# Lightning attention feeding a routed expert layer: where routing's small products stand within a step, and when the first expert's weights are asked for

## The chip, the cores and the metric

The kernel runs on one core of one Trainium2 chip. The figure of merit is device time in microseconds (us), from launch to the last instruction, of one execution; where several executions are given, their median. A profile records one further execution, instruction by instruction; its span (first to last instruction) is a little shorter than the time of that same execution.

The engines are called as in the profile: PE (matrix products; its weight loads are PEld), DVE (elementwise work and scans), ACT (scaling, copies, activations), POOL (elementwise work and indirect DMAs), SP (issues most DMAs). A name with a q, as SPq, is the engine's own instruction queue. Each engine works through its queue in order; between engines, semaphores are the only order.

## The reference

Two blocks. The first is lightning attention over 4 sequences (B), 8 heads, 768 positions and 64 channels; block by block, a decaying state `kv` carries the past:

```python
for b in range(nb):
    intra = einsum('bhic,bhjc->bhij', qb, kb) * Dmask
    intra = einsum('bhij,bhjd->bhid', intra, vb)
    inter = einsum('bhid,bhde->bhie', qb * lam_pow, kv_state)
    out[:, :, sl] = intra + inter
    kv_state = lam_block * kv_state + einsum('bhsd,bhse->bhde', kb * rev_pow, vb)
```

Its output, 3072 rows of 512 values, feeds a layer of 8 experts. Each row gets logits; its expert is the argmax where a local gate is below one half or the sequence begins, and otherwise the expert of the row before it:

```python
e = fresh_e if s == 0 or local_gate[b, s] < 0.5 else prev_e
out[b, s] = p[e] * (maximum(x[b, s] @ w1[e], 0) @ w2[e])
```

Routing is therefore a walk along each sequence, and the expert products can only start on rows whose routing is known.

## The kernel before

Attention runs in 24 steps `s` (`NS` of them): 6 blocks of 128 positions times the 4 sequences, sequence fastest, so that step `s` reads and updates the state of step `s - 4`. In step `s` the queues are filled in this order by hand (line 824 on; PE, DVE, SP and POOL have a manual schedule, ACT's order is the compiler's):

1. `loaded(s + 5)`: SP asks for the step's 1 MB of q, k, v and k again (tile `inp`, 6 buffers; L171).
2. `prepare(s + 3)`: POOL multiplies q by powers of the decay (`qd`, L178) and k likewise (`kd`, L181, not in the last block).
3. If `s` is in `QUARTERS`, SP asks for one quarter (512 KB) of the first expert's first weight matrix, `w1t[0]` (L831). In step 20 it asks for `w2t[0]` (L833) and then, with the routed expert's number, conditionally again (L701, L702); in step 23 for the second expert's (L836, L837).
4. `scores(s + 1)`: PE multiplies k and q of the next step into `ps` (L201 or L209) and DVE masks the result into `sm` (L213, two instructions, one for each half).
5. `from_state(s)`: PE multiplies `qd` with `kv` into `po` (L236); ACT decays `kv` (L240).
6. `logits` in steps 9, 13, 17, 21 (PE L316, DVE L317), then `extra_work(s, 0)`.
7. `gates` in steps 4, 8, 12, 16, 20 (PE L308), then `mix(s)`: PE multiplies `sm` with v into `po` (L249), and ACT copies it to `xc` (L252).
8. `update(s)`: PE multiplies `kd` with v into `pk` (L263); DVE adds that to `kv` (L266). None in the last block.
9. Rows go out to `x_dram`: some are turned by DVE (L294) and written in groups by four SP DMAs (`group_out`, L302; group 2 in step 13); the rows of steps 12 to 19 are turned by PE (L273) a step later and written by an ACT DMA each (L282, from step 13 on).
10. `extra_work(s, 1)`.

`extra_work` calls what the table `extras` has for that step and place. That is how routing is spread over the steps. For the first 8 tiles of rows: `fresh_experts(0)` (step 9: six DVE instructions that end in `mark`, L425), `along_sequences(0)` (PE L433 turns the marks into rows, DVE L436 and L442 carry each expert along its sequence into `run`), `experts_of(0)` (PE L449 turns `run` back, DVE L451 makes one-hot `hot`), `ranks(0)` (step 12; PE L460 and L461 read `hot`). The second part, 4 tiles, follows in steps 13 to 16. `first_tiles` (step 17) and `tokens_to_first_tiles` (step 18) are chains of small DVE instructions (L517 to L542, L558 to L530); in step 19 masks are made (L622 to L485) and multiplied (PE L641), and from the result DVE makes indices (L645 to L650) with which POOL gathers the first rows (L725). `constants_6` is four small ACT copies and two DVE instructions of one column (L377, L378).

After step 23, `first_turned` (PE L734, DVE L735) hands the first gathered tile to the first expert product, `hidden` (L753). From there the expert layer is a long stretch of PE work (L753, L759, L983, L988) to the end.

SP's and ACT's DMAs share eight completion semaphores in turn; a DMA that takes a semaphore over waits in its engine's queue for the DMA that had it before.

Of the kernel before, what the change touches and what calls it, by code (L numbers as in the profile page):

```python
# [37 lines left out]
NA = B * CA  # L38
PARTS = [(0, 8), (8, NA), (NA, NT)]
LOADS = 6  # L40
QUARTERS = [16, 17, 18, 19]
WIDE = [3, 4, 5, 7, 9, 11]
TURNED = {**{r: r + 1 for r in range(3 * B)}, 11: 13, 20: 22, 21: 23, 22: 23}
WARM = 10
# [21 lines left out]
def kernel(  # L66
# [26 lines left out]
    def w1_src(e):  # L93
        return w1[bass.ds(e, 1)].rearrange("o (t p) f -> p (o t) f", p=P)
# [278 lines left out]
    def constants_6():  # L373
        for k in range(4):
            nc.scalar.copy(dupq[:, QP * k:QP * k + QP], ident[:, :QP])
        row = ints[0][:, 2 * P:2 * P + 1]
        nc.vector.tensor_scalar(row, row, P - QP, None, ALU.bitwise_and)  # L377
        nc.vector.tensor_scalar(fourth, row, 1.0 / QP, None, ALU.mult)  # L378
# [19 lines left out]
    def pool(i):  # L398
        return pools[i == 2]

    def hot_of(i):
        lo, hi = PARTS[i]
        return hots[lo // NA][:, :, lo % NA:lo % NA + hi - lo]

    def fresh_experts(i):

        lo, hi = PARTS[i]
        n = hi - lo
        lg = lt[:, lo:hi, :E]
        if not i:  # L410
            nc.vector.memset(lt[0:1, :B, E:], -1.0)
        if i == 2:
            room = rt.tile([P, 2, NA, E], F32, name="each0", bufs=1).rearrange("p k n e -> p (k n e)")
            mx, best, mark = (room[:, n * (E + k):n * (E + k) + n] for k in range(3))
            top, mark = room[:, :n * E].rearrange("p (n e) -> p n e", e=E), mark.bitcast(BF16)[:, :n]
        else:
            mx, best = (rt.tile([P, n], F32, name=f"{k}{i}", bufs=1) for k in ("mx", "best"))
            top = rt.tile([P, n, E], F32, name=f"top{i}", bufs=1)
            mark = rt.tile([P, n], BF16, name=f"mark{i}", bufs=1)
        nows["mx", i], nows["mark"] = mx, mark  # L420
        nc.vector.tensor_reduce(mx, lg, axis=AX.X, op=ALU.max)
        nc.vector.tensor_tensor(top, lg, mx.unsqueeze(2).broadcast_to([P, n, E]), ALU.is_equal)
        nc.vector.tensor_tensor(top, top, down.unsqueeze(1).broadcast_to([P, n, E]), ALU.mult)
        nc.vector.tensor_reduce(best, top, axis=AX.X, op=ALU.max)
        nc.vector.scalar_tensor_tensor(mark, lt[:, lo:hi, E], FRESH, best, ALU.is_le, ALU.mult)  # L425

    def along_sequences(i):

        lo, hi = PARTS[i]
        n = (hi - lo) // B  # L430
        prow = pr[:B, :P * n]
        for c in range(n):
            nc.tensor.matmul(prow[:, P * c:P * c + P], lhsT=nows["mark"][:, B * c:B * c + B], rhs=identb,  # L433
                             start=True, stop=True, skip_group_check=True)
        stay = pool(i).tile([B, P * n], BF16, name=f"stay{i}", bufs=1)
        nc.vector.tensor_scalar(stay, prow, 0.0, None, ALU.is_equal)  # L436
        run = runs[i] = pool(i).tile([B, P * n], BF16, name=f"run{i}", bufs=1)
        before = 0.0
        if i:
            before = rt.tile([B, 1], F32, name="carry", bufs=1)  # L440
            nc.scalar.copy(before, runs[i - 1][:, -1:])
        nc.vector.tensor_tensor_scan(run, stay, prow, before, ALU.mult, ALU.add)  # L442

    def experts_of(i):
        lo, hi = PARTS[i]
        n = hi - lo
        pe = pr[:, P * CA:P * CA + n]
        for c in range(n // B):
            nc.tensor.matmul(pe[:, B * c:B * c + B], lhsT=runs[i][:, P * c:P * c + P], rhs=identb[:B, :B],  # L449
                             start=True, stop=True, skip_group_check=True)  # L450
        nc.vector.tensor_tensor(hot_of(i), pe.unsqueeze(1).broadcast_to([P, E, n]),  # L451
                                down.unsqueeze(2).broadcast_to([P, E, n]), ALU.is_equal)

    def ranks(i):

        lo, hi = PARTS[i]
        n, hot = hi - lo, hot_of(i)
        ptot = pr[:, :E * n].rearrange("p (e t) -> p e t", e=E)
        prank = pr[:, E * NA:E * NA + E * n].rearrange("p (e t) -> p e t", e=E)
        nc.tensor.matmul(ptot, lhsT=onesb, rhs=hot, start=True, stop=True, skip_group_check=True)  # L460
        nc.tensor.matmul(prank, lhsT=beforeb, rhs=hot, start=True, stop=True, skip_group_check=True)  # L461
        tot = pool(i).tile([P, E, n + 1], F32, name=f"tot{i}", bufs=1)
        nc.scalar.copy(tot[:, :, 1:], ptot)
        if i:
            nc.scalar.copy(tot[:, :, 0:1], counts[i - 1])
        else:
            nc.vector.memset(tot[:, :, 0:1], 0.0)
        incl = pool(i).tile([P, E, n + 1], F32, name=f"incl{i}", bufs=1)
        nc.vector.tensor_tensor_scan(incl.rearrange("p e t -> p (e t)"), go[i].rearrange("p e t -> p (e t)"),
                                     tot.rearrange("p e t -> p (e t)"), 0.0, ALU.mult, ALU.add)  # L470
        counts[i] = incl[:, :, n:]
        where = pool(i).tile([P, E, n], F32, name=f"where{i}", bufs=1)
        nc.vector.tensor_tensor(where, prank, incl[:, :, :n], ALU.add)
        nc.vector.tensor_tensor(where, where, hot, ALU.mult)
        rank = pool(i).tile([P, n], I32, name=f"rank{i}", bufs=1)
        with nc.allow_low_precision("whole numbers"):
            nc.vector.tensor_reduce(rank, where.rearrange("p e t -> p t e"), axis=AX.X, op=ALU.add)
        nc.vector.tensor_scalar(place[:, 0, lo:hi], rank, P - 1, None, ALU.bitwise_and)
        nc.vector.tensor_scalar(place[:, 1, lo:hi], rank, -P, None, ALU.bitwise_and)

    def masks(i):

        lo, hi = PARTS[i]
        lane = onehots[i] = (act if i == 2 else route).tile([P, hi - lo, P], BF16, name=f"lane{i}", bufs=1)
        nc.vector.tensor_tensor(lane, countb.unsqueeze(1).broadcast_to([P, hi - lo, P]),  # L485
                                place[:, 0, lo:hi].unsqueeze(2).broadcast_to([P, hi - lo, P]), ALU.is_equal)
# [130 lines left out]
    def brought(i, ks):  # L617

        n, (g0, g1) = NT if i else NA, span(i)
        if 0 in ks:  # L620
            hit = nows["hit"] = pools[i].tile([P, n, g1 - g0], BF16, name=f"hit{i}", bufs=1)
            nc.vector.tensor_tensor(hit, whole[:, g0:g1].unsqueeze(1).broadcast_to([P, n, g1 - g0]),  # L622
                                    nows["to"].unsqueeze(2).broadcast_to([P, n, g1 - g0]), ALU.is_equal)
        hit = nows["hit"]
        if i:
            val = w1t[2].rearrange("p t f -> p (t f)").bitcast(BF16)[:, :n * len(ks) * (g1 - g0)]
            val = nows["val"] = val.rearrange("p (n k g) -> p n k g", n=n, k=len(ks))
        else:
            val = nows["val"] = rt.tile([P, n, len(ks), g1 - g0], BF16, name=f"val{ks[0]}", bufs=1)
        for j, k in enumerate(ks):  # L630
            nc.vector.tensor_tensor(val[:, :, j], hit, parts[:, :n, k].unsqueeze(2).broadcast_to([P, n, g1 - g0]),
                                    ALU.mult)
# [155 lines left out]
    def number(k, n):  # L788
# [2 lines left out]


    extras = {
        (6, 1): constants_2, (7, 1): constants_3, (8, 1): constants_4, (9, 1): constants_5, (10, 1): constants_6,
        (9, 0): lambda: fresh_experts(0), (10, 0): lambda: along_sequences(0), (11, 0): lambda: experts_of(0),
        (12, 0): lambda: ranks(0), (13, 0): lambda: fresh_experts(1), (14, 0): lambda: (along_sequences(1), masks(0)),
        (15, 0): lambda: experts_of(1), (16, 0): lambda: ranks(1), (17, 0): first_tiles,
        (18, 0): tokens_to_first_tiles, (19, 0): lambda: (brought(0, (0, 1)), masks(1)),
        (19, 1): lambda: by_slots(0, (0, 1)), (20, 0): lambda: (ahead(0, 0), ahead(1, 1), rows_out(0)),
        (20, 1): lambda: chances(0), (21, 0): lambda: chances(1), (22, 0): lambda: brought(0, (2, 3, 4)),  # L800
# [6 lines left out]
    with tc.manual_schedule(engines={PE, DVE, SP, POOL}):  # L807
# [16 lines left out]
        for s in range(NS):  # L824
            if s + LOADS - 1 < NS:
                loaded(s + LOADS - 1)
            if s + 4 < NS and s != 1:
                prepare(s + 3)
            if s in QUARTERS:
                j = QUARTERS.index(s)  # L830
                nc.sync.dma_start(out=w1t[0][:, j], in_=w1_src(0)[:, j])  # L831
# [528 lines left out]
```

## Time and profile before

Three executions took 445.30, 445.82 and 443.42 us: median 445.3.

| | us |
|---|---|
| time of the profiled execution | 444.67 |
| its span | 442.9 |
| PE busy (matmuls) | 426.8, 96% |
| DVE busy | 287.7, 65% |
| ACT busy | 194.9, 44% |
| POOL busy | 109.0, 25% |
| first expert product starts | 98.73 |

The page draws engines, clock and DMA in 40 slices of 11.07 us. The first nine slices are attention; the granted TensorE clock was 0.995 of full speed on the mean. Times in the text are microseconds from the span's start. A wait is booked to the engine or DMA that released it last. A piece of a chain of waits is a stretch that set the start of what follows; everything else had slack.

### The profile page before, as it was taken

What the parts mean: (1) busy time and instruction counts of PE and PEld (TensorE: products, weight loads), DVE (VectorE), ACT (ScalarE), POOL (GpSimd) and SP (SyncE); (2) the same over time, 40 slices, a digit from 0 to 9 for tenths busy, and PEclk for the clock granted to TensorE, in tenths of its full rate; (3) what the DMA queues carried; (4) which work ended last, traced back from release to release, by engine and by line L of the source; (5) the groups of instructions that cost most, each with busy time, mean ns of one, the idle gap of its engine ahead of it and who ended that gap; (6) DMA issues with size and microseconds to landing.
All of it is one profiled execution on the core that took longest, in us unless ns stands there. A gap on an engine that the chain in (4) does not pass through costs nothing.

```text
span 442.9 us, 10337 instructions
## 1 busy us (share of the span) xinstructions
PE 426.8 (96%) x4094; PEld 354.4 (80%) x4094; DVE 287.7 (65%) x564; ACT 194.9 (44%) x592; POOL 109.0 (25%) x120
## 2 busy tenths in 40 slices
PE   6999899899999999999999999999999999999993
PEld 6788687677766786978777999667899999898982
DVE  5767997892239959857473785100587879878661
ACT  4245556336455105564234556451455454565110
POOL 4494584420100042205111302200202021020101
PEclk9999999999999999999999999999999999999998
DMA  7999999999999889999993799996164828370101
GB/s 262 410 366 366 361 350 323 348 341 342 347 395 392 294 304 396 399 396 404 394 398 136 255 400 367 343 368 210 40 215 146 314 81 300 128 269 3 55 1 52
DMA packets 48351, 124.84 MB, mean 282 GB/s; under 512 B 3164, under 2 KB 10844, under 8 KB 46368
## 3 DMA queue, kind: packets, MB, share of 16 engines
q1 hardware_dynamic: 42624, 108.03, 66.6%
q0 software_dynamic: 4368, 13.90, 8.9%
q10 hardware_dynamic: 1296, 2.10, 1.3%
q8 instruction: 36, 0.59, 0.5%
q14 instruction: 27, 0.22, 0.1%
HBM read 124.02 MB, written 12.91 MB: 309 GB/s over the span
## 4 chain that ended last, share of the span: by engine, by line
PE 75%; DVE 9%; DMA 8%; issue 6%; POOLq 0%; POOL 0%; ACT 0%; DVEq 0%
PE ps L753 13%; PE pk L759 12%; PE ps L983 12%; PE pk L988 11%; DMA out_dram<-y,sidxp 6%; PE po L983 5%; PE pl L988 4%; PE po L249 3%; DVE sm L213 3%; PE pr L1144 2%; PE pr L1122 2%; PE ps L209 2%; PE pk L263 1%; PE ps L201 1%; PE po L236 1%
## 5 line engine op out<-in xcount | busy, mean ns | idle before, releaser
L753 PEld LDWEIGHTS ps<-xt,w 128*128 128x128 f32 x512 | 58.2, 192 | 3.2 <-issue 2.3
L753 PE MATMUL ps<-xt,w 128*128 128x128 f32 x512 | 59.1, 276 | 0.5 <-DVE xt L735 0.5
L759 PE MATMUL pk<-w,h 128*128 128x512 f32 x128 | 56.6, 594 | 0.0
L759 PEld LDWEIGHTS pk<-w,h 128*128 128x128 f32 x128 | 23.7, 191 | 26.3 <-issue 25.5
L768 POOL DMA_INDIRECT out_dram<-y,sidx x14 | 14.0, 1001 | 105.4 <-DVE y L785 46.5
L725 POOL DMA_INDIRECT xg<-x_dram,gidx x25 | 25.8, 1033 | 56.4 <-DVE lg L739 34.1
L746 ACT COPY xp<-xlast 32x128 f32<-32x128 f32 x128 | 37.8, 296 | 1.7
L213 DVE TENSOR_TENSOR sm<-ps,mask 128x512 f32<-128x512 f32 x46 | 29.5, 681 | 7.8 <-PE ps L201 4.1
L785 DVE TENSOR_SCALAR y<-pk,gate 128x512 f32<-128x512 f32 x8 | 6.0, 744 | 43.9 <-PE pk L759 25.8
L746 ACT COPY xp<-lg 32x128 f32<-32x128 f32 x112 | 33.0, 295 | 2.6
L755 ACT ACTIVATE h<-ps 128x512 f32<-128x512 f32 x16 | 9.6, 597 | 55.2 <-PE ps L753 55.2
L178 POOL TENSOR_TENSOR qd<-inp,lamq 128x512 f32<-128x512 f32 x20 | 25.7, 1285 | 26.2 <-DMA inp<-in_qkv_dram 23.4
L983 PEld LDWEIGHTS ps<-xp,w 128*128 128x128 f32 x256 | 30.5, 192 | 1.6 <-issue 1.3
L983 PE MATMUL ps<-xp,w 128*128 128x128 f32 x256 | 31.3, 276 | 0.0
L983 PE MATMUL ps<-xs,s 128*128 128x128 f32 x256 | 31.2, 275 | 0.0
L988 PE MATMUL pk<-w,h 128*128 128x256 f32 x128 | 30.5, 381 | 0.0
L988 PE MATMUL pk<-s,hsum 128*128 128x256 f32 x128 | 30.3, 380 | 0.0
L249 PE MATMUL po<-sm,inp 128*64 128x128 f32 x384 | 27.9, 280 | 2.3 <-DVE sm L213 1.6
L983 PEld LDWEIGHTS ps<-xs,s 128*128 128x128 f32 x256 | 29.9, 192 | 0.0
L249 PEld LDWEIGHTS po<-sm,inp 128*64 128x64 f32 x384 | 21.0, 136 | 10.1 <-issue 5.8
L988 PEld LDWEIGHTS pk<-s,hsum 128*128 128x128 f32 x128 | 24.0, 190 | 3.2 <-DVE s L1071 0.2
L988 PEld LDWEIGHTS pk<-w,h 128*128 128x128 f32 x128 | 23.6, 191 | 3.3 <-issue 0.6
(282 smaller groups left out, 784.4 us busy)
## 6 DMA issues: line engine op xcount, KB each, us to landing
w<-in_w_dram SPq DMA_DIRECT2D x43, 2048.0 KB, 12.0
inp<-in_qkv_dram SPq DMA_DIRECT2D x15, 1024.0 KB, 10.8
inp<-in_qkv_dram SPq DMA_DIRECT2D x10, 512.0 KB, 8.4
x_dram<-w SPq DMA_DIRECT2D x12, 256.0 KB, 5.7
inp<-in_qkv_dram SPq DMA_DIRECT2D x4, 768.0 KB, 8.2
x_dram<-xn ACTq DMA_DIRECT2D x8, 256.0 KB, 6.8
w<-in_w_dram SPq DMA_DIRECT2D x4, 512.0 KB
x_dram<-inp SPq DMA_DIRECT2D x4, 192.0 KB, 7.8
```

The lines of the kernel that those rows point to most:

```text
L178: nc.gpsimd.tensor_tensor(qd, x[:, 0].rearrange("p (a i) -> p a i", i=P), lamq, ALU.mult)
L209: nc.tensor.matmul(ps[u][half, a, first:], lhsT=kt[rows, a, half], rhs=qt[rows, a, first:], start=True, stop=True, skip_group_check=True)
L213: nc.vector.tensor_tensor(sm[:, u], ps[u], mask[:, u], ALU.mult)
L249: nc.tensor.matmul(head(a, u), lhsT=vn[:, a, u], rhs=sm[:, u, a], start=(not c and a < 2), stop=True, skip_group_check=True)
L725: nc.gpsimd.indirect_dma_start(out=xg, out_offset=None, in_=x_dram[:n, :], in_offset=bass.IndirectOffsetOnAxis(ap=gidx[i][:, j:j + 1], axi ...
L746: copy(xt[QP * j:QP * j + QP, :, QP * k:QP * k + QP], blocks[QP * k:QP * k + QP, :, j])
L753: nc.tensor.matmul(ph[:, j], lhsT=w1t[w][:, d, P * f:P * f + P], rhs=xtt[i][:, d], start=(d == 0), stop=(d == DT - 1))
L755: nc.scalar.activation(hq[half, i], ph, ACT.Relu)
L759: nc.tensor.matmul(pys[i], lhsT=hq[f // 4, i][:, f % 4], rhs=w2t[w][:, f], start=(f == 0), stop=(f == FT - 1))
L768: apart(nc.gpsimd.indirect_dma_start(out=out, out_offset=bass.IndirectOffsetOnAxis(ap=sidx[i][:, j:j + 1], axis=0), in_=y, in_offset=None, ...
L983: nc.tensor.matmul(to[:, m], lhsT=a[:, k, P * m:P * m + P], rhs=b[:, k], start=(new and not m and not k), stop=(k == 1), skip_group_check= ...
L988: nc.tensor.matmul(to, lhsT=a[:, f], rhs=b[:, f], start=(new and not f), stop=(f == FT // 2 - 1), skip_group_check=True)
```

## The change

`along_sequences` and `experts_of` move from place 0 of their steps (ahead of `mix`) to place 1 (after `update` and the rows that go out), for both parts of the rows. `constants_6` is called just ahead of `along_sequences(0)`, in the same place of step 10 as before. `masks(0)` stays in place 0 of step 14. The four quarters of `w1t[0]` are asked for in steps 12 to 15 instead of 16 to 19. Nothing else differs.

```diff
-QUARTERS = [16, 17, 18, 19]
+QUARTERS = [12, 13, 14, 15]
...
-        (6, 1): constants_2, (7, 1): constants_3, (8, 1): constants_4, (9, 1): constants_5, (10, 1): constants_6,
-        (9, 0): lambda: fresh_experts(0), (10, 0): lambda: along_sequences(0), (11, 0): lambda: experts_of(0),
-        (12, 0): lambda: ranks(0), (13, 0): lambda: fresh_experts(1), (14, 0): lambda: (along_sequences(1), masks(0)),
-        (15, 0): lambda: experts_of(1), (16, 0): lambda: ranks(1), (17, 0): first_tiles,
+        (6, 1): constants_2, (7, 1): constants_3, (8, 1): constants_4, (9, 1): constants_5,
+        (9, 0): lambda: fresh_experts(0), (10, 1): lambda: (constants_6(), along_sequences(0)), (11, 1): lambda: experts_of(0),
+        (12, 0): lambda: ranks(0), (13, 0): lambda: fresh_experts(1), (14, 0): lambda: masks(0), (14, 1): lambda: along_sequences(1),
+        (15, 1): lambda: experts_of(1), (16, 0): lambda: ranks(1), (17, 0): first_tiles,
```

In SP's queue the order was load 17, load 18, the four writes of group 2, load 19, load 20, load 21, quarter, load 22, quarter, load 23, quarter, quarter, `w2t[0]`. It becomes load 17, quarter, load 18, quarter, the four writes of group 2, load 19, quarter, load 20, quarter, load 21, load 22, load 23, `w2t[0]` (load `n` fills `inp` for step `n`). POOL's queue is unchanged; PE and DVE execute the same instructions in another order.

## The prediction

> **What bounds the kernel now.** I read the page's slices first, to see which engine is short; then the chain of waits, to see where attention ends late; then the waits around the edited places; then the orders of DVE and POOL where the chain is DVE's.
>
> ```profile
> PE   6999899899999999999999999999999999999993
> DVE  5767997892239959857473785100587879878661
> DMA  7999999999999889999993799996164828370101
> ```
>
> PE is full nearly throughout, and from the first expert product at 98.73 us on it waits 0.5 us in all until 386 (for the first tile, L735). So the expert layer is a block of fixed length, and the change is worth what it does to the start at 98.73. In slices 1 to 9 DVE and DMA are as full as PE; the limit there has to be read step by step.
>
> The chain of waits, 36 to 64 us (start, length, what):
>
> ```profile
> 40.82 0.71 DVE sm L213 x2
> ...
> 44.53 0.81 DVE mark L425
> ...
> 46.75 1.19 DVE sm L213 x2
> ...
> 50.14 1.21 DVE sm L213 x2
> 51.34 0.04 issue
> 51.38 0.79 PE ps L209 x18
> ```
>
> From 40.82 to 51.38 (steps 9 to 12) the chain is DVE's own queue; after that PE's until 72.7 (one stall of 0.72 us at 60.44), then again mostly DVE's until 98.73.
>
> The waits in attention (total us, times, longest):
>
> ```profile
> PE pr L433 <- DVE mark L425: 1.1, 1, 1.1
> ...
> SPq L831 <- DMA x_dram<-xn: 11.1, 3, 8.2
> ```
>
> The first is PE's wait for the marks that the change takes away. The second says that a DMA in SP's queue can be held for a row write of ACT's, whose semaphore it takes over.
>
> DVE, then POOL, in step 17 (start, length, line):
>
> ```profile
> 74.08 1.22 DVE L517 TENSOR_TENSOR more<-incl,whole 128x96 f32<-128x96 f32 x1
> ...
> 75.62 0.61 DVE L537 TENSOR_TENSOR_SCAN ends<-ones,tiles 128x8 f32<-128x8 f32 x1
> ...
> 76.47 1.22 DVE L539 TENSOR_SCALAR ends<-ends 128x8 f32<-128x8 f32 x1
> 77.61 0.16 DVE L540 TENSOR_SCALAR table<-table 128x8 f32<-128x8 f32 x1
> ```
> ```profile
> 73.91 1.28 POOL L178 TENSOR_TENSOR qd<-inp,lamq 128x512 f32<-128x512 f32 x1 [6.02 <-DMA inp<-in_qkv_dram]
> 75.14 1.06 POOL L181 TENSOR_TENSOR kd<-inp,rev 128x512 f32<-128x512 f32 x1
> 76.39 1.27 POOL L178 TENSOR_TENSOR qd<-inp,lamq 128x512 f32<-128x512 f32 x1 [0.18 <-DMA inp<-in_qkv_dram]
> ```
>
> L539 and L540 are the same operation on the same shape: 1.22 and 0.16 us. The long one began just after a POOL product and ended just after it (77.69 against 77.66); so did L517 (75.30, 75.19) and L537 (76.23, 76.20). When POOL's products run is set by when `inp` lands (its bracketed waits). That is how the moved quarters can reach the critical queue, in either direction.
>
> **Part 1: marks and runs behind the update.** Step 10: PE ended `from_state` at 44.64, waited 1.11 us for the marks, then mixed. Now it mixes at once (the mask's result has stood since 42.07): `mix` 1.02 and `update` 0.56 end at 46.2, then L433. But the next thing of PE's that matters, scores for step 12, needs the `ps` that DVE's masking of step 11 releases, 46.67 to 47.94, and DVE comes to that through its own queue, unchanged up to there. After it DVE has the same instructions in another order: before, L436 and L442, then `kv`, the turn L294, L377 and L378; now `kv`, L294, L377, L378, L436, L442. Starts apart: 0.43 + 0.61 + 0.31 + 0.63 + 0.20 = 2.18 us either way, so the next masking starts at 50.05 in both. L433's result, there at 46.5, is wanted at 49.2. Step 11 likewise: `hot` (0.13) goes behind `kv` (0.33) and the turn (0.63), ending near 52.5; the reader, PE's L460, ran at 52.65. Cover: DVE's queue. If it were not the limit, the 1.11 us would be gained; if `hot` came late, up to 0.2 lost. I take 0.
>
> Steps 14 and 15: PE is the limit, and the marks were there (no wait at L433). Its instructions, 0.15 and 0.10 us, stay in the same step: 0. On DVE, `masks(0)` (1.12) now comes ahead of L436 and L442 (0.7): same sum before the next masking at 64.72, and the scores behind that stand at 67.20. Again 0.
>
> **Part 2: the quarters, in bytes.** 58 to 60 us, with loads alone in flight, moved at 414 GB/s: 0.524 MB is 1.27 us, a 1 MB load 2.53. DMA is saturated there, so two quarters ahead of load 19 cost 2.5 us of queue, which the four writes of group 2 and load 19 meet. Coming first they also mean that nothing is gained for `w1t[0]`: it was complete at 92.0 and is needed at 98.73.
>
> **Part 3: the quarters, in semaphores.** In the built program's list of waits one more SP DMA ahead of group 2 moves the turn. Now the third write of group 2 waits for the row write that ACT issues at 59.95, load 19 for the one at 64.48, load 20 for 67.93, load 22 for 72.41. Before, load 19 followed group 2 at 64.98 without such a wait. How long does a row write take? L831's three waits give 67.93 to 76.54, 72.41 to 79.07, 76.34 to 81.74: 8.6, 6.7, 5.4 us, the first behind three loads. For the one at 64.48 the ACT queue's bytes are done by 68, some 4 us. So load 19 goes out between 68.5 and 73.1; I take 70, as it will lie behind group 2's writes, as the short case did, with a quarter's tail more. A load that found the queue nearly dry, load 22, landed 7.1 us after issue with a quarter ahead of it (1.27); so alone 5.8: load 19 lands near 75.8 (bounds 74.3 and 73.1 + 9.2 = 82.3, the longest being that of loads 19 and 20) against 73.9. Load 20, issued near 72 behind a quarter, near 78.5 against 76.3; 21 near 82.5 against 78.95; 22 near 85 against 84.15.
>
> Who waits for load 19? PE's scores at 75.62, then DVE's masking, which started only at 78.42, since DVE was busy until then. Scores take 0.9, so it may land until 77.5 without cost: 1.6 us of slack left. Load 20: scores at 80.16, masking at 82.18, slack about 1 us at 78.5 to 80.3 and more. Load 21: scores at 84.82, 2.3. Load 22: scores at 89.50; its POOL product stands ahead of the gather at 86.22, which may slip by 0.1 to 1 us; the tile that it fetches is wanted at 95.92, and the gather's last bytes moved before 94. I take 0 for lateness; bounds 0 and 82.3 - 77.5 = +4.8.
>
> **Part 4: POOL's products move against DVE.** Steps 17 to 19 lost to such overlaps: L517 1.22 against 0.25 (L520, the like-sized reduction), L537 0.61 against 0.25, L539 1.22 against 0.16, L558 0.92 against 0.35 (L561 over the same elements), L649 0.60 against 0.17: 0.97 + 0.36 + 1.06 + 0.57 + 0.43 = 3.4 us, most of what four products could cost. With load 19 at 75.8, L517 to L542 would run free: eight starts of about 0.2 from 74.08 end at 75.9, `kv` (0.34) at 76.2; the masking then waits for scores, 75.8 + 0.9 = 76.7, not 78.42: a lead of 1.7. Some is lost again: `qd`, `kd` of 19 and `qd` of 20 now run 75.8 to 78.2 and 78.5 to 79.8, over L558 to L530 (eight short ones), up to 1.3; with load 21 at 82.5 its product falls on L622 to L485 (masks, 1.1 us) or on L649. I take back 1.4 of the 1.7: -0.3. Bounds: PE's own work (scores of 21 not before 83.0, if update and row turns follow at once, against 84.82 and a 0.48 stall) gives -2.3 at best; at worst, no lead and one more product's 1.3 lost.
>
> The Trainium skill, "SBUF — State Buffer", section "Who interferes with whom", says that DVE and POOL share one pair of ports as an exclusive lock and that "Issue order, not op shape, decides who blocks." The rows above agree in kind (1.22 against 0.16 us). Its summary would have one schedule off the critical path whichever can wait; this change does not choose, it lets landings decide. By the rule alone the sum would be -3.4 if every overlap went and about 0 if all came back.
>
> **Part 5: later weights.** `w2t[0]` landed at 99.0 and let `w1t[1]` go at 99.16; with the quarters done earlier it may land near 93 to 96. Its first reader is at 108.55, that of `w1t[1]` at 115.67, and PE waits for no weight there: 0.
>
> **Sum.** 0 + 0 + 0 - 0.3 + 0 on a span of 442.9: 442.6. The profiled execution's own time is 444.67 (1.8 around the span), 0.6 under the median of 445.3; I take -0.3 off the median: 445.0.
>
> **Rivals.**
> - *The 1.11 us of waiting for marks were on the path.* For: PE stood still. Against: the chain runs over DVE there. 445.3 - 1.1 - 0.3 = 443.9. Chance 0.09, within 0.5%.
> - *Overlaps mostly vanish.* Loads 19 to 21 land in gaps: -2.3, with the first rival's gain perhaps more: 443.0 down to 441.9. For: 3.4 us are lost to them now. Against: the same products must run somewhere. Chance 0.22.
> - *Loads late behind row writes (slower).* One mechanism: load 19 held for the row write of 64.48, load 20 for that of 67.93. From a landing past 77.5 each us late is a us of path. With the 8.6 us wait and a landing 7.1 after, 80.2: +2.7; at the bound +4.8: 448.0 to 450.1. For: 8.2 us were waited so before. Against: the row writes there were behind three loads. Chance 0.27.
> - *It does nothing*: landings shift within their slack and overlaps even out: 445.3. With the forecast: 0.42.
>
> **Chances and range.** A measurement of this kernel tells about 0.5%, 2.2 us, from no change: 443.1 to 447.5. Faster 0.22, same 0.09 + 0.42 = 0.51, slower 0.27. The forecast's own range, from the middle of the terms, is 443.9 to 446.6. For 8 in 10 I go into both outer cases, leaving one in ten each: 442.1 to 448.6.
>
> **What would show it.** Part 1: no PE wait at L433 in step 10, yet masking of steps 12 and 13 at 50.1 and 52.4 as before. Part 3: SP's waits for row writes move from L831 to L171 and L302, and POOL's wait for `inp` of step 19 ends near 75.8. Part 4: L517 and L539 near 0.2 us, L558 or L485 longer. Part 5: no PE wait for weights. It would be wrong if PE waits for `inp` at L209 in step 18, if the masking of step 12 starts a microsecond earlier, or if the first expert product starts over 2 us from 98.7.

## The result, and the profile after

The changed kernel took 448.0 us (median of 21 executions, 446.25 to 449.81); the kernel before, on the same chip, 445.69 (21 executions, 443.42 to 449.75). The ratio is 1.0063, 95% interval 1.0046 to 1.0080: some 2.8 us slower by the ratio (the two medians lie 2.3 us apart). The profiled execution after has a span of 446.3 us, before 442.9. The first expert product starts at 101.64, before at 98.73: 2.9 of the 3.4 us are lost ahead of it, so what has to be explained is still attention.

Timeline of the kernel after, single engines picked out (start, length, engine, line; in brackets the idle time before it and what ended that):

```profile
46.73 0.27 PE L433 MATMUL pr<-identb,mark 128*4 128x128 bf16 x2
...
75.45 0.25 DVE L517 TENSOR_TENSOR more<-incl,whole 128x96 f32<-128x96 f32 x1
...
75.74 1.27 POOL L178 TENSOR_TENSOR qd<-inp,lamq 128x512 f32<-128x512 f32 x1 [6.58 <-DMA inp<-in_qkv_dram]
...
76.02 1.02 DVE L537 TENSOR_TENSOR_SCAN ends<-ones,tiles 128x8 f32<-128x8 f32 x1
77.07 0.96 DVE L538 TENSOR_TENSOR table<-ends,tiles 128x8 f32<-128x8 f32 x1
78.07 0.17 DVE L539 TENSOR_SCALAR ends<-ends 128x8 f32<-128x8 f32 x1
...
82.11 0.90 PE L209 MATMUL ps<-inp 64*64 64x128 f32 x32 [1.39 <-DVE owner L530]
82.13 1.27 POOL L178 TENSOR_TENSOR qd<-inp,lamq 128x512 f32<-128x512 f32 x1 [4.12 <-DMA inp<-in_qkv_dram]
...
85.92 0.57 PE L209 MATMUL ps<-inp 64*64 64x128 f32 x13
86.04 1.26 POOL L178 TENSOR_TENSOR qd<-inp,lamq 128x512 f32<-128x512 f32 x1 [2.63 <-DMA inp<-in_qkv_dram]
...
88.29 0.60 PE L209 MATMUL ps<-inp 64*64 64x64 f32 x18 [1.80 <-issue]
```

The kernel before, PE at the scores of steps 20 and 21:

```profile
80.16 0.90 PE L209 MATMUL ps<-inp 64*64 64x128 f32 x32
...
84.82 0.56 PE L209 MATMUL ps<-inp 64*64 64x128 f32 x13
85.86 0.61 PE L209 MATMUL ps<-inp 64*64 64x64 f32 x18 [0.48 <-issue]
```

Five things stand in them. PE no longer waits at L433. L517 and L539 are short now (0.25 and 0.17 us, before 1.22 both), but L537 and L538 beside the next POOL products are long (before 0.61 and 0.17). Load 19 landed at 75.74, when POOL's `qd` could start; loads 20 and 21 at 82.1 and 86, against 76.39 and 78.97 before. And PE's scores for steps 20 and 21 start in the same moments as `qd` on these loads: 82.11 and 85.92, that is 1.95 and 1.10 us later than before. Fifth, within the scores of step 21 PE then stood still for 1.80 us, before for 0.48, with no releaser that the profile shows. At 82.11 the wait is booked to DVE's L530, but that began at 81.89, lasts 0.16 us and has nothing to do with `inp`; what ends at 82.1 is the load.

SP's waits, 40 to 125 us (total, times, longest):

```profile
SPq L171 <- DMA x_dram<-xn: 6.9, 3, 4.6
SPq L833 <- DMA x_dram<-xn: 6.0, 1, 6.0
...
SPq L302 <- DMA x_dram<-xn: 4.5, 1, 4.5
```

Before, it was the quarters (L831) that were held for ACT's row writes, 11.1 us in all. Now it is the loads of `inp` (L171), the fourth group's writes (L302) and `w2t[0]` (L833). The chain of waits, 66 to 92 us:

```profile
69.20 6.18 DMA x_dram<-xn
...
75.45 0.33 SPq L171
...
75.82 1.34 SPq L831
...
77.28 8.60 DMA inp<-in_qkv_dram
...
85.92 0.57 PE ps L209 x11
86.49 1.80 issue
```

Read downwards: the row write that ACT issued at 69.20 was done after 6.18 us; only then did SP issue load 20 (75.45), then the fourth quarter (75.82, 1.34 us to issue), then load 21 (77.28), which took 8.60 us, and then PE stood for 1.80 us. In the kernel before, no DMA stands in the chain between 70 and 92 us. So two things delay the loads at once: SP is *held* for a row write, and load 21 *lands slowly*, with a quarter's bytes ahead of it. The experiments try to take these apart.

The late loads are not the whole loss of this one execution. Of the 2.9 us, 1.1 are there when the scores of step 21 start; 1.3 more come from PE's longer stop within them (1.80 against 0.48), and the last 0.5 from DVE behind it (L505 lasts 1.74 us beside a product of POOL's; before, it was L501 with 1.24). Nor is it shown that all of the 1.1 comes from the loads: DVE's masking of step 18, ahead of load 19, already stood at 74.03, before at 72.66. PE had stopped for 0.60 and 1.54 us without a releaser at 55.27 and 61.00, before once for 0.72.

### The profile page after: what moved, and what is told of

Read it like the earlier page. It is cut to its first block, busy times and chain, and to the rows that moved or that the text cites. A ratio compares the mean times of both kernels' runs of the same rounds, so it can differ in the third digit from the quotient of the medians.

```text
span 446.3 us, 10338 instructions
## 1 busy us (share of the span) xinstructions
PE 429.0 (96%) x4094; PEld 356.4 (80%) x4094; DVE 287.0 (64%) x564; ACT 195.2 (44%) x592; POOL 108.2 (24%) x120
## 4 chain that ended last, share of the span: by engine, by line
PE 71%; DMA 15%; issue 6%; DVE 5%; SPq 0%; POOLq 0%; ACT 0%; POOL 0%
PE ps L753 13%; PE pk L759 12%; PE ps L983 11%; PE pk L988 10%; DMA out_dram<-y,sidxp 6%; PE po L983 4%; PE pl L988 4%; DMA w<-in_w_dram 4%; PE po L249 3%; PE ps L209 2%; PE pr L1144 2%; DMA inp<-in_qkv_dram 2%; DVE sm L213 2%; PE po L236 2%; PE pk L263 1%
## 5 line engine op out<-in xcount | busy, mean ns | idle before, releaser
L753 PEld LDWEIGHTS ps<-xt,w 128*128 128x128 f32 x512 | 58.2, 192 | 3.2 <-issue 2.3
L753 PE MATMUL ps<-xt,w 128*128 128x128 f32 x512 | 59.1, 276 | 0.5 <-DVE xt L735 0.5
L759 PEld LDWEIGHTS pk<-w,h 128*128 128x128 f32 x128 | 23.6, 190 | 26.3 <-issue 25.6
L755 ACT ACTIVATE h<-ps 128x512 f32<-128x512 f32 x16 | 9.6, 597 | 56.4 <-PE ps L753 56.4
L249 PE MATMUL po<-sm,inp 128*64 128x128 f32 x384 | 28.5, 286 | 1.3 <-DVE sm L213 0.6
L249 PEld LDWEIGHTS po<-sm,inp 128*64 128x64 f32 x384 | 21.8, 140 | 9.8 <-issue 6.8
L240 ACT ACTIVATE kv<-kv,lamq 128x64 f32<-128x64 f32 x64 | 17.4, 338 | 21.2 <-PE po L236 21.2
```

What stands on the lines that cost most here:

```text
L240: nc.scalar.mul(kv[:, a], kv[:, a], lamq[:, a, P - 1:P])
L249: nc.tensor.matmul(head(a, u), lhsT=vn[:, a, u], rhs=sm[:, u, a], start=(not c and a < 2), stop=True, skip_group_check=True)
L753: nc.tensor.matmul(ph[:, j], lhsT=w1t[w][:, d, P * f:P * f + P], rhs=xtt[i][:, d], start=(d == 0), stop=(d == DT - 1))
L755: nc.scalar.activation(hq[half, i], ph, ACT.Relu)
L759: nc.tensor.matmul(pys[i], lhsT=hq[f // 4, i][:, f % 4], rhs=w2t[w][:, f], start=(f == 0), stop=(f == FT - 1))
```

## The experiments

Each was timed against the kernel before on the same chip (6 to 12 executions; before 444.77, 445.27, 444.79 and 445.31 us in the four groups).

**1. Order or quarters?** Two kernels take one part of the change each. `e1_order` is the changed kernel with the quarters put back:

```diff
-QUARTERS = [12, 13, 14, 15]
+QUARTERS = [16, 17, 18, 19]
```

> Only the moved products (marks and runs behind the update), quarters in steps 16 to 19 as before. Theory A (the quarters make the loss): within 0.7 us of the kernel before, masking of steps 12 and 13 at the old times, and loads 20 and 21 issued at 67 to 68 us as before. Theory B (the new order makes it): about +2.8 us, the whole loss of the change.

445.3 us, ratio 1.0001 (0.9979 to 1.0022). The new order of PE's and DVE's instructions neither costs nor gains. `e2_quarters` is the kernel before with the quarters moved alone (the same two lines the other way round):

> Only the quarters in steps 12 to 15, products where they were. Theory A: +2 to +3.5 us, load 20 issued near 75 us and landing past 80. Theory B: within 0.7 us of the kernel before.

448.11 us, ratio 1.0072 (1.0048 to 1.0096). The quarters make the whole loss. Its chain of waits, 70 to 92 us, has the same links as that of the whole change:

```profile
69.54 5.47 DMA x_dram<-xn
...
76.00 10.90 DMA inp<-in_qkv_dram
```

Here load 21 took 10.90 us, and PE's waits name the loads: `PE ps L209 <- DMA inp<-in_qkv_dram` 2.6 us in two waits, 0.87 for load 20 and 1.73 for load 21. The scores of step 21 start at 86.95, 2.1 us later than before, and no stop without a releaser stands in them; 1.6 us more are lost behind them, most of it in DVE instructions beside POOL's (L505 2.02 us).

**2. Hold or bytes, first try.** `e3_turn` asks for an eighth of each quarter early and for the rest where it was:

```diff
+            if s + 4 in QUARTERS:
+                j = s + 4 - QUARTERS[0]
+                nc.sync.dma_start(out=w1t[0][:, j, :P], in_=w1_src(0)[:, j, :P])
...
-                nc.sync.dma_start(out=w1t[0][:, j], in_=w1_src(0)[:, j])
+                nc.sync.dma_start(out=w1t[0][:, j, P:], in_=w1_src(0)[:, j, P:])
```

> Order of before; in steps 12 to 15 SP asks for one eighth of each quarter (64 KB), in steps 16 to 19 for the other seven eighths: the turn of the semaphores moves, nearly no bytes come earlier. Here the list of waits puts load 20 behind the row write of step 14 and load 21 behind that of step 15. Theory turn (waits for row writes delay loads 20 and 21): load 20 issued at 70 to 72 and load 21 past 74, +1 to +3 us. Theory bytes (1 MB of weights in a full queue delays everything behind): within 0.7 us of before.

444.9 us, ratio 1.0008 (0.9981 to 1.0035): no loss that the timing shows. Load 20 went out at 69.80 (before at 67.00), held for no row write. It was the last of the four eighths (step 15) that waited 5.0 us for one, until 75.52, and load 21, behind it in SP's queue, went out only at 75.96; before, at 67.99. It landed at 82.16, 3.2 us later than before, and PE did not wait for it. So here load 21 was held nearly as long as in the changed kernel (77.28), but without the quarters' bytes, and the loss forecast for the turn, 1 to 3 us, did not come: 0.4 by the ratio, at most 1.6. Of a long hold of load 20 the run tells nothing.

`e4_bytes` gives the early quarters to POOL's queue, which takes no turn with SP and ACT:

```diff
-            if s in QUARTERS:
-                j = QUARTERS.index(s)
-                nc.sync.dma_start(out=w1t[0][:, j], in_=w1_src(0)[:, j])
+            if s + 4 in QUARTERS:
+                j = s + 4 - QUARTERS[0]
+                nc.gpsimd.dma_start(out=w1t[0][:, j], in_=w1_src(0)[:, j])
```

> Order of before; the quarters are asked for in steps 12 to 15 by POOL's queue, whose DMAs take none of the eight semaphores of SP and ACT: bytes come early, the turn up to load 21 is as before. Theory turn: within 0.8 us of before, loads 20 and 21 issued near 67 to 68. Theory bytes: +2 to +3 us, load 19 landing 2 us or more later than 73.9, PE waiting at the scores of steps 18 to 20. A third theory, that PE's stalls without a releaser (0.72 us at 60.4, 0.48 at 85.4 before; 0.60, 1.54 and 1.80 after) grow with what else is in the DMA engines: they are as long here as after the change.

448.54 us, ratio 1.0066 (1.0043 to 1.0089), but for another reason. Its timeline, POOL and DVE:

```profile
59.52 0.76 POOL L831 DMA_DIRECT2D w<-in_w_dram  x1
...
59.88 4.54 DVE L425 SCALAR_TENSOR_TENSOR mark<-lt,best 128x4 bf16<-128x4 f32 x1
60.30 1.28 POOL L178 TENSOR_TENSOR qd<-inp,lamq 128x512 f32<-128x512 f32 x1
61.52 1.06 POOL L181 TENSOR_TENSOR kd<-inp,rev 128x512 f32<-128x512 f32 x1
62.50 0.60 POOL L831 DMA_DIRECT2D w<-in_w_dram  x1
63.12 1.27 POOL L178 TENSOR_TENSOR qd<-inp,lamq 128x512 f32<-128x512 f32 x1
```

DVE's mark, about 1 us in the kernel before, lasted 4.54 us, as long as POOL worked without a gap, and ended with POOL's last product. PE waited 3.3 us for it. The quarters' issues had closed the gaps between POOL's products; the run tells nothing of the bytes.

**3. How many quarters, and where?** In `x1_early_two` quarters 1 and 2 are asked for in steps 12 and 13, in `x2_late_two` in steps 14 and 15, 3 and 4 in steps 18 and 19 in both; in `x5_all_late` all four in step 19, behind load 23. All have the order of before; each entry is a quarter and its columns:

```diff
+ASKS = {12: [(0, 0, 1024)], 13: [(1, 0, 1024)], 18: [(2, 0, 1024)], 19: [(3, 0, 1024)]}
...
-            if s in QUARTERS:
-                j = QUARTERS.index(s)
-                nc.sync.dma_start(out=w1t[0][:, j], in_=w1_src(0)[:, j])
+            for j, lo, hi in ASKS.get(s, ()):
+                nc.sync.dma_start(out=w1t[0][:, j, lo:hi], in_=w1_src(0)[:, j, lo:hi])
```

> Order of before; quarters 1 and 2 in steps 12 and 13, quarters 3 and 4 in steps 18 and 19. If the two early quarters do it, by 2.5 us of bytes ahead of group 2 and load 19: +1.5 to +2.8 us. If only the quarters that stand between loads 19 and 21 matter: at most +0.7 us, and no wait of the products for loads 20 and 21.

446.62 us, ratio 1.0025 (1.0008 to 1.0043). It lost about 1.1 us, between the two figures given beforehand, so it decides for neither. Held for a row write was load 19, issued at 70.07; PE waited 1.12 us for it.

> Order of before; quarters 1 and 2 in steps 14 and 15, that is between loads 19, 20 and 21, quarters 3 and 4 in steps 18 and 19. If bytes and turn between loads 19 and 21 do it: +1.5 to +3 us, with load 21 landing 8 us or more after its issue. If the early two are needed to start the lateness: at most +0.7 us.

447.0 us, ratio 1.0025 (1.0002 to 1.0047), about 1.1 us again, and again between the two figures. Load 21 landed at 84.0, 7 us or so after its issue near 77, but PE shows no wait for loads 19 to 21; where its loss arises is not settled.

> Order of before; all four quarters in step 19, behind load 23. Nothing of them stands ahead of loads 19 to 21, so by the theory of late loads: -0.5 to +0.5 us against before, no wait of the products for loads 20 and 21. A rival, that the quarters cost their bytes wherever they are put, since the queue is full until the last load: +1 us or more, through load 23 or the shared weights.

445.91 us, ratio 1.0005 (0.998 to 1.0029). The same bytes behind the last load cost 0.2 us by the ratio, at most 1.3, as the theory of late loads has it; the rival of bytes that cost wherever they are put forecast 1 us or more and is left with the edge of the interval. An eighth of each, two quarters and four ahead of the last loads thus give 0.4, 1.1 and some 3 us: it is no matter of one place alone.

**4. The hold without the bytes.** In `x9_turn_only` the four early DMAs are under a condition that never holds, and the real quarters stay in steps 16 to 19:

```diff
+    never = route.tile([1, 1], I32, name="never")
+    nc.vector.memset(never, 0)
...
+            if s + 4 in QUARTERS:
+                j = QUARTERS.index(s + 4)
+                if not j:
+                    zero = nc.values_load(never[0:1, 0:1], engines=[SP], min_val=0, max_val=1,
+                                          skip_runtime_bounds_check_because="a constant")
+                nc.sync.dma_start(out=w1t[0][:, j], in_=w1_src(0)[:, j], cond=zero > 0, cond_hint=True)
```

> The four DMAs of steps 12 to 15 stand in SyncE's queue where the changed kernel has them and take the same turns among the semaphores, but under a condition that never holds, so that they move no bytes; the real quarters are asked for in steps 16 to 19 as before; order of before. If the turn alone costs the time (load 20 behind a row write that lands late): +1 to +2.8 us against before, load 20 of group 2 issued near 75 and load 21's product waiting. If the loss needs turn and bytes together: at most +0.7 us; load 20 is still issued near 72 to 75, but load 21 lands within some 6 us of its issue, as in the kernel before, where it is 8.6 with the quarters ahead of it.

447.67 us, ratio 1.0040 (1.0010 to 1.0070). Load 20 was held as in the changed kernel (issued at 74.56), yet landed at 79.35, load 21 at 81.5, and no product waited for them. But the real quarters moved the turn further down: load 22 was now held until 85.96, and the scores waited 2.1 us for it; later PE waited 1.76 us for the gathered rows and 1.21 us for weights of the second expert. `y9_turn_late_bytes` takes that away: the same, with all four real quarters in step 19:

```diff
+            if s == 19:
+                for j in range(4):
+                    nc.sync.dma_start(out=w1t[0][:, j], in_=w1_src(0)[:, j])
```

> As the run with the turn alone (four DMAs in steps 12 to 15 that move nothing), but all four real quarters are asked for in step 19, behind load 23, so that every load has the turn that it has in the changed kernel, load 22 too, and no quarter stands ahead of a load; order of before. If the time goes where turn and bytes meet (load 20 late by the row write, load 21 late by the bytes on top): at most +0.8 us, loads 20 and 21 issued near 75 and landed by 82, with no wait of the scores for them. If the turn alone costs it: +1.5 us or more, and a wait for load 20 or 21.

447.12 us, ratio 1.0059 (1.0036 to 1.0083): more than the +0.8 that I allowed. Yet in its timeline the loads come in time (its kernel is two lines longer there, so that its L755 is L753 of before and its L551 is L549):

```profile
74.73 0.35 SPq L171 DMA_DIRECT2D inp<-in_qkv_dram  x1
...
79.61 0.90 PE L209 MATMUL ps<-inp 64*64 64x128 f32 x32 [0.78 <-DVE late L551]
79.63 1.30 POOL L178 TENSOR_TENSOR qd<-inp,lamq 128x512 f32<-128x512 f32 x1 [3.36 <-DMA inp<-in_qkv_dram]
...
117.73 7.38 PE L755 MATMUL ps<-xt,w 128*128 128x128 f32 x64 [1.56 <-DMA w<-in_w_dram]
```

Load 20 landed by 79.6, load 21 by 82.3. PE's wait of 0.78 us ends with load 20, but the scores behind it start at 79.61, earlier than before (80.16). The first expert product started at 99.22, half a microsecond behind that of before. The largest loss stands at 117.73: PE waits 1.56 us for weights of the second expert. Load 23 was held to about 84.7 here, the quarters behind it went out at 85.04, and SP came to the second expert's weights at 103.90, before at 99.16.

Two more runs are to separate this. `u3_load20_held` has such empty DMAs in steps 12, 13 and 14, `u1_control` one in step 12 (`NEVER = [12, 13, 14]` and `[12]`), both with all quarters in step 19. By the program's list of waits, load 20 is held in the first and not in the second:

> Order of before; DMAs that move nothing in steps 12, 13 and 14, all four quarters in step 19 behind load 23. By the program's list of waits load 20 stands behind the row write of step 14's turn as in the changed kernel, and loads 21 to 23 behind writes of group 2 that are long done. So load 20 is held to about 75 and nothing else is. Theory that a late load costs only where bytes keep it from landing: at most +0.8 us over the kernel with one such DMA in step 12, no load in the chain of waits between 60 and 92. Theory that the hold alone costs: +1.5 us or more over it, and a wait of the scores for load 20 or 21.

> Order of before; one DMA that moves nothing, in step 12, all four quarters in step 19 behind load 23. Loads 19 to 21 are not held for a row write; load 22 stands behind one, as in the run with all quarters in step 19. It is the control for the condition itself: if a DMA under a condition costs nothing, the time of the run with all quarters in step 19, -0.5 to +0.8 us against before; if the condition brought the losses of the two runs with the turn alone, +1.5 us or more here too.

`u1_control` took 445.92 us, ratio 1.0017 (0.9992 to 1.0042): the condition itself costs little or nothing. `u3_load20_held` took 447.1, ratio 1.0061 (1.0029 to 1.0094), against both of my theories: load 20 was issued at 74.81 and landed by 81.15, no score waited for loads 20 and 21, and the second expert's weights cost it only 0.20 us. Its profile loses 2.07 us to the control's by the first expert product (100.32 against 98.25), and it was behind before load 20 was due: the first row write after 60.2 us went out at 67.27, in the control at 63.94. The timeline of PE in `u3_load20_held`, then in `u1_control`:

```profile
62.45 0.53 PE L236 MATMUL po<-qd,kv 64*64 64x128 f32 x7 [1.81 <-issue]
```
```profile
60.62 0.45 PE L236 MATMUL po<-qd,kv 64*64 64x128 f32 x7 [0.17 <-issue]
```

This is a stop that thirteen of the fourteen profiles here have in the same place, with changing length (see the end); it stands 12 us ahead of the held load and is not the hold. Behind it the granted clock was 0.59 in 62 to 66 us, in the control 1.00, and the products of step 14 (L249) lasted 1.98 us instead of 1.09. So the three runs with the hold and without the bytes are slower by 0.4 to 0.6%, but in their profiles not by waiting for loads 20 and 21. What a hold costs through load 20 alone stays open; for load 21 there is `e3_turn`.

**5. The bytes without the hold.** `z1_bytes_no_turn` repeats `e4_bytes` where POOL has a gap of 6 us, in step 15, so that its issues can't close up with its products:

```diff
-            if s in QUARTERS:
-                j = QUARTERS.index(s)
-                nc.sync.dma_start(out=w1t[0][:, j], in_=w1_src(0)[:, j])
+            if s == 15:
+                for j in range(4):
+                    nc.gpsimd.dma_start(out=w1t[0][:, j], in_=w1_src(0)[:, j])
```

> Order of before; all four quarters asked for by GpSimd's queue in step 15, in its idle time of 6 us ahead of load 19's products, so that they take no turn among the semaphores of SyncE and ScalarE and SyncE holds nothing for them: their whole bytes, about 5 us of the queues, stand ahead of loads 20 and 21. If turn and bytes are needed together: at most +0.8 us, load 21 landed by 84. If the bytes alone cost it: +1.5 us or more, with a wait of the scores for load 20 or 21. If GpSimd's issues hold VectorE's port again, a VectorE instruction near 68 to 72 is several us long, and the run tells nothing of the bytes.

446.78 us, ratio 1.0041 (1.0022 to 1.0059): the bytes without the hold cost 1.8 us. No DVE instruction was stretched (the masking at 72.34 stood at 72.12 in `u1_control` and 72.45 in `y9_turn_late_bytes`). The chain of waits, 55 to 92 us:

```profile
67.17 13.53 DMA inp<-in_qkv_dram
...
80.84 0.89 PE ps L209 x22
...
84.91 5.03 DMA x_dram<-xn
```

Load 20 was issued at 67.17, as before the change (67.0), and was held for nothing. The quarters went out behind it, from 67.51 to 69.9, by POOL's queue. The load took 13.53 us to land; before, 9.3. The 4.2 us more are most of the four quarters' 5.1 us (four times 1.27): bytes that another queue asks for just after a load make it late too. PE waited 1.77 us for it.

That wait is little of what this execution lost, though. The scores of step 20 started 0.7 us later than before (80.84 against 80.16), those of step 21 no later (84.51 against 84.82). The chain goes on through a row write: ACT issued it at 84.91 and took up its next work only at 90.12 (before, 88.29); beside that, PE stopped for 1.95 us without a releaser within the scores of step 21. The first expert product started at 101.42, 2.7 us later than before. Whether the quarters' bytes made the row write's hold or the stop longer, no run here shows. Against `x5_all_late`, which moves the same bytes behind the last load and leaves loads 20 and 21 without a hold as well, the difference is the place of the bytes and the queue that asks for them. No run was faster than the kernel before.

## Why the prediction was wrong

**What bounds the kernel now, and the block behind it: right.** From the first expert product to the end the spans without a wait for weights are within 0.6 us of each other (442.9 - 98.73 = 344.2 before, 446.3 - 101.64 = 344.7 after).

**Part 1, marks and runs behind the update, 0: right.** The wait at L433 of step 10 is gone and nothing follows from it: maskings of steps 12 and 13 at 49.62 and 51.89, forecast 50.1 and 52.4. The half microsecond was there ahead of the edited place (`kv` of step 9 at 45.17, before 45.62). `e1_order` measures it: 1.0001. The rival that had the 1.11 us on the path falls.

**Part 3, the quarters in semaphores: the step that failed.** It had the right waits and the right landing of load 19 (75.8 forecast, 75.74 measured). It failed at "Load 20, issued near 72 behind a quarter, near 78.5", with the row write that holds it (67.93 to 72) taken at some 4 us. That value came from the row write that holds load 19, whose bytes I judged done early, and for that one it was near enough (issued at 65.71, load 19 out at 69.34); the three that the same paragraph read off took 8.6, 6.7 and 5.4 us. In the change the one ahead of load 20 took 6.18, and it was issued at 69.20, 1.3 us later than before, behind PE's stops without a releaser. So load 20 went out at 75.45 and landed at 82.1, 3.6 us later than forecast and beyond the slack to 80.3 that the text gave it. (By the paragraph's own 7.1 us for a load behind a quarter, 72 would have given 79.1 and not 78.5, still within the slack.) Load 21 landed at 85.9, 3.4 later than "near 82.5", beyond its 2.3. The term "I take 0 for lateness" measured 1.95 us at the scores of step 20 and 1.10 at those of step 21, in `e2_quarters` 2.1 at the latter.

The sum also has no term for the stop of PE within the scores of step 21: it read its 0.48 us and let it stand, and it came out at 1.80. What sets that length is open.

The rival *Loads late behind row writes* was the case that came: 448.0 to 450.1 forecast, 448.0 measured. Its mechanism was half right and its figure partly luck. It priced load 19, which was in time; the loads' lateness gives at most 1.1 of the 2.9 us in this profile; and it left out that the quarters' bytes delay a load as well.

**Part 2, the quarters in bytes: about the right price, wrong reach.** 1.27 us each is near what `z1_bytes_no_turn` shows (4.2 us later for four). But two of them were charged to group 2 and load 19 only, and for load 21 the quarter ahead of it was given too little: 8.60 us from issue to landing in the change and 10.90 in `e2_quarters`, in both beyond the 7.1 read off for a load behind a quarter. By the timing of `z1_bytes_no_turn` the bytes without the hold make 1.8 of the 2.8 to 3.2 us; the rest is not split further here, as the hold without bytes was not measured cleanly.

The Trainium skill, "DMA: Bandwidth & Descriptors", section "Queues, rings and completion order", says that a DMA's completion signal lands only after every earlier write of the same DMA engine, whichever queue that came from. It would have spoken against 4 us: a row write of 256 KB issued behind loads and quarters is not signalled done before them. The rows agree in kind, 6.18 and 5.47 us for it and 3.6 for the one ahead of load 19, against 0.6 us that its bytes take at 414 GB/s; no run here separates the signal from the bytes.

**Part 4, -0.3 from overlaps: the lead came, smaller, and was lost again.** As forecast, L517 and L539 became short, but L537 (1.02) and L538 (0.96) grew long. From the masking of step 18 to that of step 19 DVE took 4.94 us, before 5.76: a lead of 0.8 instead of 1.7, and it went in waiting for load 20. L649 (1.28, before 0.60) followed, and L505 (1.74) took the place of L501 (1.24 before). POOL's products do move with the landings, but DVE's losses move along.

**Part 5, later weights, 0: right.** PE waits for no weight in the changed kernel.

**Does nothing, overlaps vanish:** both needed loads within their slack, which loads 20 and 21 overran.

## What to carry to other kernels

A transfer that is not urgent is safe behind the last urgent one (`x5_all_late`). Elsewhere, in a stretch where the queues are full, the loads beside it come later, here by 4.2 us for 2 MB, even those asked for just before it by another queue; the slack has to be checked for the last load of the row and not for the first. A wait of an issuing queue should be priced with the rows of its kind that were issued under the same traffic (here 5.4 to 8.6 us), and not with a guess below them. Where a kernel's stage has a few microseconds of slack, spend them once: here row writes and quarters each used the slack of loads 20 and 21. And one profile is one execution: its stops without a releaser alone added up to between 0.2 and 5.3 us ahead of the first expert product, so a difference of 3 us between two profiles has to be followed piece by piece before it is given to one cause.

## What the runs showed of the hardware that I had not expected

- PE stops without a releaser at regular places of the program. Thirteen of the fourteen profiles have one after nine of sixteen products of L236 in step 14 (0.17 to 1.81 us; 0.72 before, 1.54 after; `z1_bytes_no_turn` has none there), and six have one within the scores of step 21 (L209; 1.80 us in the changed kernel, 1.95 in `z1_bytes_no_turn`, 0.43 to 0.93 in the other four). Counted in PE's timelines from 36 us to the first expert product, all but two short ones (`z1_bytes_no_turn`, near 92 us) lie 126 matrix products apart, or a multiple of that, give or take one. That looks like a supply of instructions in blocks of one size; no run here tests it. Nor is it shown that the stops grow with the quarters' bytes: up to the first expert product they add up to 4.36 us after the change and 1.20 before, but to 5.27 in `x5_all_late`, which lost nothing that its timing shows, and `e2_quarters` has none in the scores of step 21.
- The granted clock fell after PE's stops, and in the changed kernel that is not the cause of the loss. A window of the kernel after (us, busy time of each engine, clock, DMA share, GB/s):

```profile
86.00:92.00 6.00, 4.20 (x68) 2.51 (x70) 4.04 (x13) 0.98 (x3) 4.28 (x4) 0.81 1.02 393
```

  The 0.81 is the clock, after 1.80 us of standing still; before it was 1.00 there. The chain runs over DVE behind that place. `e3_turn` shows 0.72 in the same window and lost nothing, and `z1_bytes_no_turn` 1.00 and lost 1.8 us. In step 14, where PE sets the pace, it did count in `u3_load20_held` (0.59 after a stop of 1.81 us), while `x5_all_late` kept 1.00 after a stop of the same length.
- An instruction of DVE can last over several instructions of POOL (`e4_bytes`: 4.54 us over five). The Trainium skill, "SBUF — State Buffer", section "Who interferes with whom", says of DVE's 2-port modes that the engine that issues first keeps the shared ports for its whole instruction. Here DVE seems not to have got them between POOL's instructions either, as long as POOL left no gap; that it was the ports is not shown.
